# FFN output stores from the scalar engine's queue, x's split pinned in order, and the local attention's way through HBM in two reads

## The chip, the cores and the metric

The kernel runs on one core of a Trainium2 chip. Times are device microseconds (us) of one execution. The engines are PE (matrix products), DVE (VectorE), ACT (ScalarE), POOL (GpSimd) and SP (SyncE, which here does nothing but issue DMA transfers). Each engine works through its own instructions in order.

## The reference

Attention over 8 batches and 8 heads, 576 positions, 64 dimensions, feeds a feed-forward network (FFN) over 4608 tokens:

```python
q_d, k_d, v_d = means over 4 neighbouring positions of q, k, v
out_up    = repeat(softmax(q_d @ k_d.T / 8) @ v_d, 4)             # "far"
mask      = |i - j| < 4
out_local = softmax(where(mask, q @ k.T / 8, -1e9)) @ v           # "local"
x = transpose(out_up + out_local) as (4608, 512)
h = x @ w_in                         # 512 x 2048
r = maximum(h, 0)
out = (s * r * r + b) @ w_out        # 2048 x 512
```

All values are fp32.

## The kernel before

**The FFN** works through 18 tiles of 256 tokens. A tile has 8 panels of 256 hidden columns; a pair (tile, panel) is a step. To keep fp32 accuracy, each operand is split into a high and a low part of the matrix engine's format, and each product is three matmuls: high x high, high x low, low x high. For x these parts are `xh` (a copy with rounding, on ACT) and `xl` (the difference, on DVE), made by `split_x(t)` for a whole tile `t` (L752, L753). A step consists of G, the first products into `ph` (L771); R, on ACT: Relu, Square and the cast to the high part `gh` or `gb` (L786 to L788); V, on DVE: the low part `gl` or the second half of `gb` (L793); and H, the second products into `po` (L852 to L854), which lag G by some three steps. When a tile's H are done, DVE evicts `po` into `os` in two halves (L826), and each half goes to HBM as a store of 128 x 512 values (L829), issued by SP at that place.

**Attention.** The first 28 steps, up to about 240 us, follow an order written out by hand. Behind it a loop emits, per step, some products of G and H, then `finish` (R and V), then a share of the remaining attention (`advance`, a generator that is drawn from as fast as the next batches' x are due), and then `split`, which calls `split_x(t + 1)` once step 5 of tile `t`, for `t` from 3 to 16, is reached. From these emissions a scheduler with a timeline simulation sets each engine's order, so an instruction can stand ahead of where the program emitted it.

The attention left for the loop is that of batches 3 to 7, in ten groups of two head pairs (`two_pairs`), each of two halves. A half of the local part is: seven products `pr` on POOL (L672) of queries with shifted keys, both in `lqk`, a single buffer that is loaded again (768 KB) once the half's last `pr` has read it; seven sums `st` on DVE (L674); a softmax over the seven; and the weighted values, `pv` on DVE (L701), added into `acc` on POOL or DVE (L702). The far part (`tqk`, `qd`, `dmx`, `pd`) runs between these as a chain of its own, whose own transposition goes through HBM too (`away` and `pd`, L605 to L620).

At a group's end the local part has positions on partitions, while x wants model columns there. Two DVE transposes of 32 x 32 blocks (L712) write `ft`, two transfers write that to HBM as `away` (L717, 288 KB each), eight read it back, moved between partitions, into the same `ft` (L722, 72 KB each). POOL then adds the two `ft` into x (L730); these two adds are kept in `late` and emitted behind the last `pr` of the next group's first half. `ft` and `pv` share one pair of buffers. All transfers are issued by SP, in the order of its queue. The words `ft` and `away` name tiles of the far part as well; lines tell them apart.

Of the kernel before, what the change touches and what calls it, by code (L numbers as in the profile page):

```python
# [11 lines left out]
F32 = mybir.dt.float32  # L12
# [4 lines left out]
ALU = mybir.AluOpType  # L17
AX = mybir.AxisListType

P = 128  # L20
# [22 lines left out]
CH = 9  # L43
# [43 lines left out]
def attention_ffn_kernel(ctx, tc, qk, vw_in, vr_in, vdm, qkn, vn, w_in, w_out, s_in, b_in, out):  # L87
    nc = tc.nc
# [3 lines left out]
    def pool(name, bufs, gap=0):  # L92
# [11 lines left out]
    two = pool("two", 2)  # L104
    far_off = ctx.enter_context(
        tc.tile_pool(name="far_off", bufs=2, space=bass.MemoryType.DRAM))
# [5 lines left out]
    def bank(i, shape, name):  # L112
        return ps.tile(shape, F32, tag=f"k{i}", name=name)
# [536 lines left out]
    def two_pairs(b, g, dn):  # L650

        at = GROUPS.index((b, g))
        i = 0

        def far():
            nonlocal i
            if i % 3 == 2:
                next(dn)
            if i == 17:
                load_far(2 * at + 2, ("qk",))  # L660
            i += 1

        acc = None
        st = bank(7, [P, 2, P], "st")
        for h in range(2):
            half = 2 * at + h
            lqk, lv = near_in[half, "lqk"], near_in[half, "lv"]
            ls = take(st[:, h], 0, [P, CH, NO])
            sums = st[:, h, 64 : 64 + CH]
            for o in range(NO):  # L670
                pr = two.tile([P, CH, D], F32, tag="pl", name="pr")
                nc.gpsimd.tensor_tensor(  # L672
                    pr, lqk[:, 0:CH], lqk[:, CH + o : 2 * CH + o], ALU.mult)
                nc.vector.tensor_reduce(ls[:, :, o], pr, AX.X, ALU.add)  # L674
                if o == NO - 1:
                    load_near(half + 1, "lqk")
                    far_values(half)
                    while late:
                        late.pop()()
                far()  # L680
                yield
            row = lambda t: t.unsqueeze(2).to_broadcast([P, CH, NO])
            nc.vector.tensor_tensor(ls, ls, omask, ALU.add)
            lr = two.tile([P, 2, CH], F32, tag="lr", name="lr")
            nc.vector.tensor_reduce(lr[:, 0], ls, AX.X, ALU.max)
            nc.vector.tensor_tensor(ls, ls, row(lr[:, 0]), ALU.subtract)
            nc.scalar.activation(ls, ls, AF.Exp, scale=SCALE)
            nc.vector.tensor_reduce(sums, ls, AX.X, ALU.add)
            nc.vector.tensor_scalar(sums, sums, 1e-9, None, ALU.add)
            nc.vector.reciprocal(lr[:, 1], sums)  # L690
            nc.vector.tensor_tensor(ls, ls, row(lr[:, 1]), ALU.mult)
            far()
            yield
            acc = acc or two.tile([P, CH, 2, D], F32, tag="qk", name="acc")
            for o in range(NO):
                w = ls[:, :, o : o + 1].to_broadcast([P, CH, D])
                if o == 0:
                    nc.vector.tensor_tensor(acc[:, :, h], lv[:, 0:CH], w, ALU.mult)
                else:
                    pv = two.tile([P, CH, D], F32, tag="pv", name="pv")  # L700
                    nc.vector.tensor_tensor(pv, lv[:, o : o + CH], w, ALU.mult)  # L701
                    (nc.vector if o % 3 == 1 else nc.gpsimd).tensor_tensor(  # L702
                        acc[:, :, h], acc[:, :, h], pv, ALU.add)
                if o == NO - 1:
                    load_near(half + 1, "lv")
                far()
                yield
        x = xt[b]
        moved, away = [], []
        for h in range(2):  # L710
            ft = two.tile([P, 2, CH * 32], F32, tag="pv", name="ft")
            nc.vector.transpose(  # L712
                ft.rearrange("p e (i b) -> p e i b", i=CH),
                acc[:, :, h].rearrange("p i (e a) -> p e i a", e=2))
            moved.append(ft)
            away.append(far_off.tile([P, 2, CH * 32], F32, name="away"))
            nc.sync.dma_start(away[h], ft)  # L717
        load_far(2 * at + 3, ("qk",))
        yield
        for u in range(2):  # L720
            for e in range(4):
                nc.sync.dma_start(  # L722
                    moved[u][32 * e : 32 * e + 32],
                    away[e // 2][64 * u : 64 * u + 64, e % 2].rearrange("(r a) n -> a r n", r=2))
        yield

        def add():
            for u in range(2):
                xv = x[:, 2 * g + u].rearrange("p (r b i) -> p r b i", r=2, b=32)
                nc.gpsimd.tensor_tensor(  # L730
                    xv, moved[u].rearrange("p r (i b) -> p r b i", i=CH), xv, ALU.add)
            complete.update((b, 2 * g + u) for u in range(2))

        late.append(add)
        yield
# [4 lines left out]
    def split_x(t):  # L740
        tags = ("os", "xl2") if t == 2 else ("xh", "xl")
        xh, xl = (home[tag].tile([P, HP, TB], F32R, tag=tag, name=name)
                  for tag, name in zip(tags, ("xh", "xl")))
        t0 = t * TB
        while t0 < (t + 1) * TB:
            b = t0 // S
            while (b, HP - 1) not in complete:
                next(gen)
            n = min((t + 1) * TB, (b + 1) * S) - t0
            src = xt[b][:, :, t0 - b * S : t0 - b * S + n]  # L750
            dst = slice(t0 - t * TB, t0 - t * TB + n)
            nc.scalar.copy(xh[:, :, dst], src)  # L752
            nc.vector.tensor_tensor(  # L753
                xl[:, :, dst], src, xh[:, :, dst].bitcast(F32), ALU.subtract)
            t0 += n
        xs[t] = (xh, xl)

# [3 lines left out]
    acc = {}  # L761
# [59 lines left out]
    def evict_half(t, m):  # L821
        if m == 0:
            pool, tag = (xp, "xh") if t < 2 else (xp1, "os")
            held[t] = pool.tile([P, 2, DM], F32, tag=tag, name="os")
        os_ = held[t] if m == 0 else held.pop(t)
        nc.vector.scalar_tensor_tensor(  # L826
            os_[:, m], oacc[t][m], sb_s, bias, ALU.mult, ALU.add)
        r0 = TB * t + P * m
        nc.sync.dma_start(out[r0 : r0 + P, :], os_[:, m])  # L829

    def evict(t):
        for m in range(2):
# [200 lines left out]
                    chain_end = i  # L1033

    def finish(st):
        with tc.high_priority():
            next(streams["R"])
            next(streams["V"])
        advance(st + 0.5)


# [40 lines left out]
    def advance(st):  # L1082
        nonlocal done
        while done < target(st):
            with tc.high_priority(offset=300 if done < NY[1] else 60 if done < NY[1] + NY[2] else 0):
                if next(gen, "end") == "end":
                    break
            done += 1
# [85 lines left out]
```

## Time and profile before

| | |
|---|---|
| median of 3 runs | 943.72 us (942.95 to 945.33) |
| the profiled execution | 944.6 us |
| its span, first to last instruction | 942.8 us |
| granted clock of PE, mean over the span | 0.995 |
| PE, DVE, ACT, POOL busy | 908.2, 654.9, 463.6, 451.8 us |
| bytes moved by DMA | 105.09 MB |
| last instructions of attention | x adds at 780.54 and 782.62 us |

A row of the timeline reads: start, duration, engine, line, operation, output<-input, shape, count, and in brackets how long the engine sat idle before it and what it waited for. In the lists of waits a row reads: who waited, for whom, us in total, times, longest. A row with `SPq` is an issue in SP's queue, and its duration is what the issue took, not the transfer. In the list of transfers the columns are count, size and median us from issue to landing.

### The profile page before, as it was taken

To read this page: it belongs to the slowest core of one execution; us is meant where nothing else is said; L and a number is where in the kernel's file an instruction comes from. 1 tells how busy PE (TensorE), PEld (TensorE's weight loads), DVE (VectorE), ACT (ScalarE), POOL (GpSimd) and SP (SyncE) were. 2 spreads that over 40 slices of the span, in tenths; PEclk is the share of its full clock that TensorE was granted. 3 is DMA by queue.
4 is the path that set the end of the run, shared out by engine and by line. 5 is a ranking of instruction groups with operands and counts; after the bars stand their busy time and mean duration, and the time that the engine had idled before them with its cause. 6 is when DMAs were issued, how large, how long until landed. Compare 5 with 4: busy or idle time off the path is not lost.

```text
span 942.8 us, 18601 instructions
## 1 busy us (share of the span) xinstructions
PE 908.2 (96%) x7106; PEld 815.3 (86%) x7106; DVE 654.9 (69%) x1134; ACT 463.6 (49%) x1073; POOL 451.8 (48%) x461
## 2 busy tenths in 40 slices
PE   6799999999999998999999999999999999999998
PEld 5688888788899888999988988989998989999997
DVE  9999999854588887887888778777968672111111
ACT  7977774466455534454544344345534443233331
POOL 6401120010467878687887677768886831000000
PEclk9999999999999999999999999999999999999999
DMA  9855413123234535434443435154434310000000
GB/s 315 279 163 193 148 47 120 46 88 98 90 113 132 157 100 158 131 118 131 138 148 99 146 101 167 56 181 125 144 100 161 85 61 26 23 1 24 1 23 23
DMA packets 60505, 105.09 MB, mean 111 GB/s; under 512 B 20480, under 2 KB 34048, under 8 KB 60416
## 3 DMA queue, kind: packets, MB, share of 16 engines
q1 hardware_dynamic: 60416, 103.90, 35.1%
q8 instruction: 56, 0.92, 0.4%
q14 instruction: 33, 0.27, 0.1%
HBM read 84.85 MB, written 19.02 MB: 110 GB/s over the span
## 4 chain that ended last, share of the span: by engine, by line
PE 42%; POOL 21%; DVE 15%; DMA 12%; issue 5%; ACT 3%; SPq 2%; DVEq 0%; POOLq 0%; ACTq 0%
PE ph L771 19%; POOL pr L672 11%; POOL acc L702 7%; PE po L852 6%; PE po L853 6%; PE po L854 6%; DMA lqk<-in_qkn_dram 4%; DVE pv L701 2%; DMA tqk<-in_qk_dram 2%; DVE st L674 2%; DMA away<-ft 2%; SPq L722 1%; DVE acc L702 1%; PE ol L481 1%; DMA ft<-away 1%
## 5 line engine op out<-in xcount | busy, mean ns | idle before, releaser
L771 PE MATMUL ph<-xh,wi 128*128 128x256 f32 x2176 | 412.6, 280 | 7.3 <-DVE gl L793 3.9
L771 PEld LDWEIGHTS ph<-xh,wi 128*128 128x128 f32 x2176 | 346.3, 189 | 18.0 <-DVE gl L793 6.1
L771 PE MATMUL ph<-xl,wi 128*128 128x256 f32 x1152 | 321.2, 279 | 0.2
L672 POOL TENSOR_TENSOR pr<-lqk 128x576 f32<-128x576 f32 x140 | 203.9, 1478 | 68.2 <-DMA lqk<-in_qkn_dram 44.3
L771 PEld LDWEIGHTS ph<-xl,wi 128*128 128x128 f32 x1152 | 218.8, 190 | 7.8 <-DVE xl L911 0.4
L786 ACT ACTIVATE ph<-ph 128x512 f32<-128x512 f32 x144 | 83.7, 581 | 258.3 <-PE ph L771 252.7
L852 PE MATMUL po<-wo,gh 128*128 128x512 f32 x416 | 166.7, 401 | 0.3
L854 PE MATMUL po<-wo,gl 128*128 128x512 f32 x416 | 163.1, 392 | 0.8 <-DVE gl L793 0.7
L853 PE MATMUL po<-wo,gh 128*128 128x512 f32 x416 | 163.4, 393 | 0.0
L674 DVE TENSOR_REDUCE st<-pr 128x9 f32<-128x576 f32 x140 | 105.6, 754 | 45.4 <-POOL pr L672 43.9
L702 POOL TENSOR_TENSOR acc<-acc,pv 128x576 f32<-128x576 f32 x80 | 114.7, 1433 | 40.0 <-DVE acc L702 22.7
L793 DVE TENSOR_TENSOR gl<-ph,gh 128x512 fp32r<-128x512 f32 x104 | 70.9, 682 | 85.5 <-ACT gh L788 85.5
L701 DVE TENSOR_TENSOR pv<-lv,st 128x576 f32<-128x576 f32 x120 | 87.8, 747 | 25.7 <-POOL acc L702 21.6
L314 POOL TENSOR_TENSOR dq<-vt 80x64 f32<-80x64 f32 x58 | 21.8, 388 | 174.4 <-PE up L385 172.9
L854 PEld LDWEIGHTS po<-wo,gl 128*128 128x128 f32 x416 | 78.3, 188 | 19.2 <-DVE gl L793 2.1
L852 PEld LDWEIGHTS po<-wo,gh 128*128 128x128 f32 x416 | 78.2, 188 | 13.3 <-issue 0.8
L853 PEld LDWEIGHTS po<-wo,gh 128*128 128x128 f32 x416 | 78.5, 189 | 11.4 <-issue 0.2
L787 ACT ACTIVATE ph<-ph 128x512 f32<-128x512 f32 x144 | 83.8, 582 | 4.0
L788 ACT CAST gh<-ph 128x512 fp32r<-128x512 f32 x104 | 61.1, 587 | 20.3 <-PE po L853 18.2
L852 PE MATMUL po<-wo,gb 128*128 128x512 f32 x160 | 63.2, 395 | 2.9 <-DVE os L826 1.7
L853 PE MATMUL po<-wo,gb 128*128 128x512 f32 x160 | 62.9, 393 | 0.0
L854 PE MATMUL po<-wo,gb 128*128 128x512 f32 x160 | 62.5, 391 | 0.0
(175 smaller groups left out, 1188.4 us busy)
## 6 DMA issues: line engine op xcount, KB each, us to landing
tqk<-in_qk_dram SPq DMA_DIRECT2D x30, 584.0 KB, 4.3
lqk<-in_qkn_dram SPq DMA_DIRECT2D x20, 768.0 KB, 4.4
lv<-in_vn_dram SPq DMA_DIRECT2D x20, 480.0 KB, 3.5
out_dram<-os SPq DMA_DIRECT2D x34, 256.0 KB, 2.1
wst<-in_moe_w_in_dram SPq DMA_DIRECT2D x7, 1024.0 KB, 5.8
wst<-in_moe_w_out_dram SPq DMA_DIRECT2D x7, 1024.0 KB, 5.1
away<-ft SPq DMA_DIRECT2D x20, 288.0 KB, 2.8
ft<-away SPq DMA_DIRECT2D x80, 72.0 KB, 2.0
```

The source lines that it names most:

```text
L672: nc.gpsimd.tensor_tensor(pr, lqk[:, 0:CH], lqk[:, CH + o : 2 * CH + o], ALU.mult)
L674: nc.vector.tensor_reduce(ls[:, :, o], pr, AX.X, ALU.add)
L701: nc.vector.tensor_tensor(pv, lv[:, o : o + CH], w, ALU.mult)
L702: (nc.vector if o % 3 == 1 else nc.gpsimd).tensor_tensor(acc[:, :, h], acc[:, :, h], pv, ALU.add)
L771: nc.tensor.matmul(ph[:, j], wi[p][:, s, k, f], xk[:, k], start=k == 0 and s == 0 and xk is xh, stop=k == NK - 1 and s == 1)
L786: nc.scalar.activation(ph, ph, AF.Relu)
L787: nc.scalar.activation(ph, ph, AF.Square)
L788: nc.scalar.copy(gh, ph)
L793: nc.vector.tensor_tensor(gl, acc.pop((t, p)), gh.bitcast(F32), ALU.subtract)
L852: nc.tensor.matmul(po[m], gh[:, j, ms], wo[p][:, 0, j], start=first, stop=False)
L853: nc.tensor.matmul(po[m], gh[:, j, ms], wo[p][:, 1, j], start=False, stop=False)
L854: nc.tensor.matmul(po[m], gl[:, j, ms], wo[p][:, 0, j], start=False, stop=last)
```

## The change

Three edits.

1. *Stores.* A finished half tile is put on a list, `to_store`. For tiles from the third on, the list is emptied in the next step's `finish`, behind that step's R and V, by DMA issues from ACT's queue, held behind ACT's last emitted instruction by a scheduling dependency (`behind`). The first two tiles' stores, and those of the last tile (another function), stay in SP's queue.
2. *Split.* `xh` is held behind ACT's and `xl` behind DVE's last emitted instruction, so they stay where the program emits them in relation to that.
3. *The local part's return.* One `away` of [4, 128, 288] per group. `turn(h)` transposes half `h` and writes it as four transfers of 72 KB, one for each 32 partitions. It is called for the first half within the second half's `pr` (behind the third), and for the second at the group's end. Two reads of 288 KB then fetch both into two new tiles, `moved`.

```diff
+        away = far_off.tile([4, P, CH * 32], F32, name="away")
+
+        def turn(h):
+            ft = two.tile([P, 2, CH * 32], F32, tag="pv", name="ft")
+            nc.vector.transpose(
+                ft.rearrange("p e (i b) -> p e i b", i=CH),
+                acc[:, :, h].rearrange("p i (e a) -> p e i a", e=2))
+            for r in range(4):
+                nc.sync.dma_start(
+                    away[r, 64 * h : 64 * h + 64].rearrange("(e a) n -> a e n", e=2),
+                    ft[32 * r : 32 * r + 32])
...
+                if h == 1 and o == 2:
+                    turn(0)
...
-        moved, away = [], []
-        for h in range(2):
-            ft = two.tile([P, 2, CH * 32], F32, tag="pv", name="ft")
-            nc.vector.transpose(
-                ft.rearrange("p e (i b) -> p e i b", i=CH),
-                acc[:, :, h].rearrange("p i (e a) -> p e i a", e=2))
-            moved.append(ft)
-            away.append(far_off.tile([P, 2, CH * 32], F32, name="away"))
-            nc.sync.dma_start(away[h], ft)
+        turn(1)
         load_far(2 * at + 3, ("qk",))
         yield
+        moved = []
         for u in range(2):
-            for e in range(4):
-                nc.sync.dma_start(
-                    moved[u][32 * e : 32 * e + 32],
-                    away[e // 2][64 * u : 64 * u + 64, e % 2].rearrange("(r a) n -> a r n", r=2))
+            moved.append(two.tile([P, 2, CH * 32], F32, tag="pv", name="moved"))
+            nc.sync.dma_start(moved[u], away[2 * u : 2 * u + 2].rearrange("r p n -> p r n"))
         yield
...
-            nc.scalar.copy(xh[:, :, dst], src)
-            nc.vector.tensor_tensor(
-                xl[:, :, dst], src, xh[:, :, dst].bitcast(F32), ALU.subtract)
+            with behind(nc.scalar.engine):
+                nc.scalar.copy(xh[:, :, dst], src)
+            with behind(nc.vector.engine):
+                nc.vector.tensor_tensor(
+                    xl[:, :, dst], src, xh[:, :, dst].bitcast(F32), ALU.subtract)
...
-        nc.sync.dma_start(out[r0 : r0 + P, :], os_[:, m])
+        to_store.append(((nc.sync if t < 2 else nc.scalar), out[r0 : r0 + P, :], os_[:, m]))
+        if t < 2:
+            store(1)
+
+    to_store = []
+
+    def store(count):
+        for _ in range(count):
+            engine, dst, src = to_store.pop(0)
+            engine.dma_start(dst, src)
...
     def finish(st):
+        ready = len(to_store)
         with tc.high_priority():
             next(streams["R"])
             next(streams["V"])
+            with behind(nc.scalar.engine):
+                store(ready)
         advance(st + 0.5)
```

The change adds 12 lines ahead of L672, so lines move: `pr` is L684 behind it, the x add L735, `xh` L758, the casts L795, the stores L845, the writes L673, the reads L729.

How the scheduler's orders differ is shown at three places. The first is POOL's queue in the first half of the second group: that half's `pr`, `vt` of the far part, the first group's two adds into x, then `pr` of the next half, whose `lqk` is loaded behind the last `pr` of this one. Before:

```order
L672 TENSOR_TENSOR pr<-lqk 128x576 x4
L310 TENSOR_TENSOR vt<-tvd 80x256
L672 TENSOR_TENSOR pr<-lqk 128x576
L730 TENSOR_TENSOR x<-ft,x 128x576 x2
L672 TENSOR_TENSOR pr<-lqk 128x576 x2
L702 TENSOR_TENSOR acc<-acc,pv 128x9x64
```

And with the change:

```order
L684 TENSOR_TENSOR pr<-lqk 128x576 x4
L735 TENSOR_TENSOR x<-moved,x 128x576 x2
L684 TENSOR_TENSOR pr<-lqk 128x576
L310 TENSOR_TENSOR vt<-tvd 80x256
L684 TENSOR_TENSOR pr<-lqk 128x576 x2
L315 TENSOR_TENSOR dq<-vq 64x64 x2
```

The two adds (`x`) have moved from behind the half's last `pr` to ahead of it.

The second is SP's queue at the end of the first group, from the local part's last write to the load of the next `lqk`. Before (the rows of L717 and L722 are the local part's, those of L609, L614 and L620 the far part's):

```order
L717 DMA away<-ft 128x576
L722 DMA ft<-away 32x2x288 x2
L717 DMA away<-ft 128x576
L609 DMA away<-ft 96x288
L609 DMA away<-ft 96x192
L722 DMA ft<-away 32x2x288 x6
L614 DMA pd<-away 32x3x96
L636 DMA lqk<-in_qkn_dram 128x1536
L614 DMA pd<-away 32x3x96
L614 DMA pd<-away 16x3x96
L620 DMA pd<-away 32x3x48 x4
```

And with the change:

```order
L673 DMA away<-ft 32x2x288 x4
L729 DMA moved<-away 128x2x288
L609 DMA away<-ft 96x288
L729 DMA moved<-away 128x2x288
L609 DMA away<-ft 96x192
L614 DMA pd<-away 32x3x96 x2
L614 DMA pd<-away 16x3x96
L620 DMA pd<-away 32x3x48 x4
L636 DMA lqk<-in_qkn_dram 128x1536
```

Eight reads have become two, and the `lqk` load now stands behind all reads of `pd`. The four writes of the group's first half now stand further up, after an earlier `lv` load:

```order
L636 DMA lv<-in_vn_dram 128x960
L673 DMA away<-ft 32x2x288 x4
L156 DMA tqk<-in_qk_dram 128x1168
L156 DMA tvr<-in_vr_dram 128x256
L636 DMA lqk<-in_qkn_dram 128x1536
L609 DMA away<-ft 96x288
```

The third is ACT's queue around the split of the tile with index 6 (its first piece, 192 tokens), by the softmax's exponential `st` of the same half as a mark. Before:

```order
L788 CAST gb<-ph 128x512
L786 ACTIVATE ph<-ph 128x512
L752 CAST xh<-x 128x4x192
L787 ACTIVATE ph<-ph 128x512
L788 CAST gh<-ph 128x512
L687 ACTIVATE st<-st 128x63
L786 ACTIVATE ph<-ph 128x512
L787 ACTIVATE ph<-ph 128x512
```

And with the change:

```order
L845 DMA out_dram<-os 128x512 x2
L793 ACTIVATE ph<-ph 128x512
L794 ACTIVATE ph<-ph 128x512
L795 CAST gh<-ph 128x512
L701 ACTIVATE st<-st 128x63
L793 ACTIVATE ph<-ph 128x512
L794 ACTIVATE ph<-ph 128x512
L795 CAST gb<-ph 128x512
L793 ACTIVATE ph<-ph 128x512
L794 ACTIVATE ph<-ph 128x512
L795 CAST gh<-ph 128x512
L758 CAST xh<-x 128x4x192
```

`xh` stood ahead of `st` and within a step; it now stands two steps behind `st`, after a step's cast. The two stores of a finished tile stand between two steps, each issued once its half is in `os`; with the waits listed, each also waits for one of eight DMA semaphores, which ACT's stores share with SP's transfers: the one transfer that used the semaphore last must have landed.

## The prediction

> **What bounds the kernel now.** I read the busy table first, then the chain of work that ended last, then what the matmul engine (PE) waited for, then single instructions around those waits. The busy row and the chain:
>
> ```profile
> PE 908.2 (96%) x7106; PEld 815.3 (86%) x7106; DVE 654.9 (69%) x1134; ACT 463.6 (49%) x1073; POOL 451.8 (48%) x461
> PE 42%; POOL 21%; DVE 15%; DMA 12%; issue 5%; ACT 3%; SPq 2%; DVEq 0%; POOLq 0%; ACTq 0%
> ```
>
> PE is busy for 908.2 of 942.8 us, so 34.6 us is everything a change of order could win. The chain runs through attention (POOL, DVE, DMA) all the same: while attention and FFN share the chip, some of PE's products wait for an x that is late. The change touches the time from 240 us on, when the hand-written plan is over, and in that stretch PE's waits are few:
>
> ```profile
> PE ph L771 <- DVE gl L793: 3.9, 3, 2.3
> PE ph L771 <- ACT xh L752: 2.6, 1, 2.6
> PE po L852 <- DVE os L826: 1.7, 1, 1.7
> PE up L547 <- ACT ph L786: 1.4, 2, 0.7
> PE po L852 <- DVE dsm L596: 1.2, 1, 1.2
> PE up L547 <- DMA pd<-away: 0.6, 1, 0.6
> PE ph L771 <- DVE gb L793: 0.6, 1, 0.6
> ```
>
> Columns: total us, times, longest, for 240 to 790 us. They sum to 12.0 us. Behind 790 PE never waits:
>
> ```profile
> 360.00:384.00 24.00, 21.26 (x124) 18.87 (x124) 17.59 (x33) 9.23 (x18) 17.05 (x13) 0.93 0.42 121
> 792.00:816.00 24.00, 24.00 (x162) 21.96 (x162) 5.44 (x7) 8.11 (x14) 0.00 (x0) 1.00 0.06 23
> ```
>
> Columns: length, busy PE, PEld, DVE, ACT, POOL, granted clock. The first window has a second loss, a clock of 0.93 behind the wait for xh:
>
> ```profile
> 369.00:372.00 3.00, 3.00 (x17) 2.91 (x16) 2.86 (x7) 0.00 (x0) 0.31 (x1) 0.63 1.04 341
> 372.00:375.00 3.00, 3.00 (x21) 2.87 (x20) 1.72 (x3) 1.35 (x3) 3.00 (x3) 0.81 0.19 75
> 621.00:624.00 3.00, 1.79 (x6) 1.60 (x7) 2.90 (x6) 0.00 (x0) 1.10 (x1) 0.72 0.50 170
> 624.00:627.00 3.00, 3.00 (x20) 2.90 (x20) 2.92 (x5) 0.00 (x0) 2.39 (x3) 0.71 0.51 136
> ```
>
> Lost at the first place: 3 x 0.37 + 3 x 0.19 = 1.7 us; at the second 3 x 0.28 + 3 x 0.29 = 1.7. These follow PE's two longest waits (2.6 and 2.3 us); so each of the two is worth about 4 us, not 2.5. [...]
>
> So at most 12.0 + 2 x 1.7 = 15.4 us can be won, and each microsecond that an x comes later at a place with no slack is lost in full.
>
> **Term 1, the stores.** 30 stores (15 tiles x 2) go from SP's queue to ACT's, behind the next step's casts. ACT's room (its wait for PE between 240 and 790), and ACT at the one long wait of its own that I tie to PE:
>
> ```profile
> ACT ph L786 <- PE ph L771: 157.3, 64, 7.2
> 541.15 0.20 ACT L589 ACTIVATE dmx<-dmx 96x3 f32<-96x3 f32 x1 [4.46 <-DVE dmx L588]
> 548.28 0.39 PE L771 MATMUL ph<-xh,wi 128*128 128x256 f32 x1 [1.30 <-DVE gl L793]
> ```
>
> ACT pays an issue each, 0.37 us by the rows below, 30 x 0.37 = 11 us, and these lie in the 157.3 us: cost 0, with the cover gone 0.37 us a store. But ACT's queue is in order, and the order of the change shows each store waiting for the last user of its DMA semaphore, mostly a transfer of SP's. Behind a store stand the next step's Relu, Square and Cast and so PE's products. ACT's 4.46 us at 541 put the two Relu, Square and Cast behind it late, and PE lost 1.30 us at 548.28. Bounds 0 and 3 such places, 3.9; I take +0.5, nearer to 0 since a store comes a whole step after its tile is evicted. The room in SP's queue is the gain:
>
> ```profile
> 624.96 1.43 POOL L672 TENSOR_TENSOR pr<-lqk 128x576 f32<-128x576 f32 x1
> 626.25 0.37 SPq L829 DMA_DIRECT2D out_dram<-os  x1
> ...
> 627.69 0.37 SPq L829 DMA_DIRECT2D out_dram<-os  x1
> 628.11 3.25 SPq L722 DMA_DIRECT2D ft<-away  x7
> 631.46 0.37 SPq L636 DMA_DIRECT2D lqk<-in_qkn_dram  x1
> ```
>
> POOL's last pr ends at 626.39; the load of the next lqk could go then, and goes 5.1 us later, behind two stores and eight reads. This is the worst of the ten groups. With 2 reads and no stores ahead of it some 4 us come back, here, to attention. [...]
>
> But x is not late after 622. One wait for x reaches PE, at 367.83; four more stay on ACT (next term). So this 4 us moves no PE product: 0 on the path, unless x comes to be late there.
>
> **Term 2, x's split.** Before, the scheduler put xh ahead of its place where ACT had room, and ACT then sat waiting for POOL's x:
>
> ```profile
> ACT xh L752 <- POOL x L730: 14.7, 5, 6.6
> L753 DVE TENSOR_TENSOR xl<-x,xh 128x1024 fp32r<-128x1024 f32 (+3 forms) x19 | 25.3, 1337 | 11.7 <-ACT xh L752 11.6
> ```
>
> Pinned behind step 5 of the tile before, both come later and these waits shrink. What of it reaches PE: xl at 513.38 (1.32 us) stood ahead of the gb for which PE waited 0.6 us (the last row of PE's waits). The other two rows are for term 4:
>
> ```profile
> 513.38 1.32 DVE L753 TENSOR_TENSOR xl<-x,xh 128x1024 fp32r<-128x1024 f32 x1
> ...
> 620.18 0.75 DVE L529 TENSOR_REDUCE qd<-tqk 128x144 f32<-128x576 f32 x1 [1.75 <-DMA tqk<-in_qk_dram]
> ...
> 622.21 0.48 PE L771 MATMUL ph<-xh,wi 128*128 128x256 f32 x1 [2.29 <-DVE gl L793]
> ```
>
> I take -0.6. From below -1.3 (the 548 wait too), from above +1.3: a pinned xl can stand ahead of another gl.
>
> **Term 3, the local part's return.** Issues per group stay 10, 4 + 4 writes and 2 reads for 2 writes and 8 reads, but behind the last transpose only 6 are left. By the 0.37 to 0.46 us (3.25 / 7) of an issue above, the last read goes some 4 x 0.4 = 1.6 us sooner. Where does that help? Only where POOL's x waits for it, and at PE's one wait for x it does not:
>
> ```profile
> 359.80 2.82 POOL L672 TENSOR_TENSOR pr<-lqk 128x576 f32<-128x576 f32 x2
> 362.58 1.75 POOL L730 TENSOR_TENSOR x<-ft,x 128x576 f32<-128x576 f32 x1
> ...
> 365.64 1.70 POOL L730 TENSOR_TENSOR x<-ft,x 128x576 f32<-128x576 f32 x1
> 367.37 1.35 ACT L752 CAST xh<-x 128x256 fp32r<-128x256 f32 x2 [2.97 <-POOL x L730]
> 367.83 0.38 PE L771 MATMUL ph<-xh,wi 128*128 128x256 f32 x1 [2.59 <-ACT xh L752]
> ```
>
> No DMA is named ahead of the x adds: POOL is full with pr, and x comes when its place in POOL's order comes. So an earlier read gives 0 here, and what decides is when POOL gets this far. That is set one group earlier, and there the order changes against the kernel: the two x adds of the first group, behind the last pr before, now stand ahead of it.
>
> ```profile
> 306.35 0.74 DVE L712 STREAM_TRANSPOSE ft<-acc 128x576 f32<-128x576 f32 x1
> 312.22 1.44 POOL L672 TENSOR_TENSOR pr<-lqk 128x576 f32<-128x576 f32 x1
> 313.61 4.14 POOL L730 TENSOR_TENSOR x<-ft,x 128x576 f32<-128x576 f32 x2
> 319.72 3.29 POOL L672 TENSOR_TENSOR pr<-lqk 128x576 f32<-128x576 f32 x2 [1.97 <-DMA lqk<-in_qkn_dram]
> lqk<-in_qkn_dram SPq DMA_DIRECT2D x20, 768.0 KB, 4.4
> away<-ft SPq DMA_DIRECT2D x20, 288.0 KB, 2.8
> ft<-away SPq DMA_DIRECT2D x80, 72.0 KB, 2.0
> ```
>
> The last pr (312.22) frees lqk's only buffer. Before, the adds ran while the next lqk was on its way; now they run ahead of its load. The way of it: the last transpose ends at 307.1; four writes issue in 1.6 us and land 2.0 (72 KB) to 2.8 us later; two reads of 288 KB issue in 0.8 and land 2.0 to 2.8 later: the first x add starts, 0.4 ahead of the second's data, between 313.1 and 314.7. Two adds of 1.75, the pr 1.4, the load 4.4: the next pr starts at 322.4 to 324.0, 2.7 to 4.3 us behind 319.72. POOL's rows up to 367 then stand much as before, so PE's wait for x becomes 2.6 + 2.7 to 2.6 + 4.3. I take +3.5. Below, 0, if the attention chain has room before 367 that I don't see.
>
> Later groups have the same flip (x adds ahead of a half's last pr: 4 of 20 before, 9 after; 5 x 1.75 = 8.8 us of cover lost), against which stands SP's relief (the 4 us of the seventh group). After 368 the x adds end well ahead of their tiles' first products, so I count 0 for both.
>
> **Term 4, shuffled waits.** DVE's and POOL's order changes nearly everywhere, and the rest of the 12.0 us (gl 3.9 with its 1.7 of clock, os 1.7, up 2.0, dsm 1.2: 10.5) hangs on which DVE instruction stands ahead of a gl or an eviction. The wait at 622 had gl behind the reduce qd, which itself waited 1.75 us for a load. Such a meeting is drawn again. Between -10.5 and about as much again I take a quarter off, -2.5: the load queue that made the dearest one gets shorter.
>
> **Sum**, against the profiled execution (944.6, its span 942.8 plus 1.8): 944.6 + 0.5 - 0.6 + 0 + 3.5 - 2.5 = 945.5. The median shown, 943.72, is 0.9 below that execution, so 944.6 in its terms; I say 944.5, no change.
>
> **The rivals.**
>
> *A, x waits no more.* Were x's adds released by the transfers, or the first half's earlier send to take the first group's pipeline along, the 2.6 us at 367.83 goes with its 1.7 of clock, the 0.56 with it, and the 622 wait by SP's relief with its clock (2.3 + 1.7): -8.9, 934.8; with one of the two places alone -4.5, 939. For it: the reads do land sooner, SP has 5.1 us to give. Against it: the rows at 362 to 367 name no DMA. Chance 0.34.
>
> *B, lqk behind the x adds.* The upper end of term 3 and nothing from term 4: POOL's x adds of the first group delay the load by 4.3 us, the wait at tile 6 becomes 6.9, and its half clock lasts for one window more (+1.7): 943.7 + 4.3 + 1.7 = 949.7. It decides once the reads land later than POOL is done with the four pr ahead of the adds. For it: the order is fixed and POOL cannot pass a waiting add. Against it: DVE reduces those pr meanwhile, and a later half may catch up. Chance 0.21.
>
> *C, ACT stuck at a store.* Three or four stores wait over 4.5 us for a transfer of SP's and PE pays 1.3 each: 943.7 + 5 = 948.7. Against it: ACT waited 6.6 us for x at one place before with no wait of PE behind it. Chance 0.08.
>
> **How the numbers follow.** 0.3% (2.8 us) is about what a measurement here can tell from no change. Forecast 0.37, A 0.34, B and C 0.29: faster 0.35, same 0.36, slower 0.29 with the forecast's own edges. The range reaches to the end of A and of B, 935 to 950; the forecast's own is 941 to 947.
>
> **What would show it.** Right: PE's wait for xh at tile 6 is longer than 2.6 us; in the first group POOL shows x, then pr, then a wait for lqk of more than 1.97 us; SP's gap of 5.1 us from a last pr to its lqk load falls under 2; ACT's issue of stores shows no PE wait within 6 us. Wrong: xh's wait gone (A), or a row of ACT waiting for a DMA ahead of a Relu that PE waits for (C).

## The result, and the profile after it

The changed kernel took 950.9 us (median of 4 runs, 950.38 to 951.79) against 943.9 us before: 1.0074 times as long, 95% interval 1.0056 to 1.0091. Measured again beside other kernels it was 950.23 us against 944.51, 1.0062 (1.0044 to 1.0080). The forecast was 944.5 and no change, the range 935 to 950: the change is slower by 6 to 7 us, just outside the range. Rival B, at 949.7, came nearest. A second profile of the changed kernel is used below as well.

The page of the changed kernel: busy times, chain, and two groups.

```profile
PE 907.8 (96%) x7106; PEld 815.3 (86%) x7106; DVE 652.9 (69%) x1134; ACT 463.0 (49%) x1073; POOL 451.4 (48%) x461
...
PE 41%; POOL 24%; DVE 16%; DMA 12%; issue 5%; SPq 1%; ACT 1%; DVEq 0%; POOLq 0%; ACTq 0%
...
L684 POOL TENSOR_TENSOR pr<-lqk 128x576 f32<-128x576 f32 x140 | 205.2, 1487 | 73.2 <-DMA lqk<-in_qkn_dram 53.8
...
L716 POOL TENSOR_TENSOR acc<-acc,pv 128x576 f32<-128x576 f32 x80 | 115.2, 1440 | 49.5 <-DVE acc L716 34.3
```

No engine has more to do: PE 907.8 us where it had 908.2, DVE 652.9 for 654.9. What grew is waiting. POOL's wait for `lqk` went from 44.3 to 53.8 us, and POOL's share of the chain from 21 to 24%. What PE waited for from 240 to 800 us (before: 12.0 us in all):

```profile
PE ph L778 <- ACT xh L758: 4.7, 1, 4.7
PE ph L778 <- DVE gb L800: 3.2, 3, 1.3
PE po L868 <- DVE os L833: 3.1, 3, 2.5
PE up L547 <- DMA pd<-away: 1.9, 2, 1.2
PE ph L778 <- DVE gl L800: 1.5, 2, 0.9
PE ph L778 <- DVE xl L760: 1.2, 2, 0.6
PE po L868 <- ACT ph L793: 0.7, 1, 0.7
PE up L547 <- issue: 0.2, 1, 0.2
```

That is 16.5 us. The windows say where. Before and after, 300 to 390, 390 to 660 and 660 to 801 us (length, then PE's busy time; the granted clock is the third value from the end of a row):

```profile
300.00:390.00 90.00, 86.42 (x561) 78.46 (x561) 71.93 (x124) 41.19 (x103) 71.53 (x67) 0.98 0.44 134
390.00:660.00 270.00, 263.43 (x1723) 238.63 (x1722) 215.29 (x373) 120.70 (x294) 207.59 (x183) 0.99 0.42 129
660.00:801.00 141.00, 138.69 (x918) 126.21 (x917) 96.88 (x166) 61.35 (x139) 87.84 (x77) 1.00 0.31 96
```

```profile
300.00:390.00 90.00, 82.79 (x527) 74.92 (x526) 70.64 (x117) 36.95 (x89) 68.46 (x61) 0.96 0.39 121
390.00:660.00 270.00, 264.94 (x1758) 240.78 (x1757) 211.99 (x368) 122.62 (x295) 209.60 (x188) 1.00 0.43 130
660.00:801.00 141.00, 136.73 (x898) 123.35 (x897) 100.49 (x176) 61.69 (x147) 89.38 (x79) 1.00 0.34 102
```

Adding the busy time spent at half clock, taken from windows of 3 us (as in the prediction: length times the missing clock), PE lost what the table shows. In the traces of before and after the clock is either 1.00 or 0.50, and from 240 to 800 us it is 0.50 in four stretches of 3.41 us each: before from 369.76 and 622.34 us on, with the change from 336.98 and 374.53. Such a stretch, 1.7 us of lost clock, is a half-clock window in what follows.

| us lost by PE: idle + half clock | before | after | after, second profile |
|---|---|---|---|
| 300 to 390 | 3.6 + 1.7 | 7.2 + 3.4 | 9.2 + 3.4 |
| 390 to 660 | 6.6 + 1.7 | 5.1 + 0 | 4.7 + 0 |
| 660 to 802 | 2.3 + 0 | 4.3 + 0 | 3.7 + 0 |
| sum | 15.9 | 20.0 | 21.0 |
| span | 942.8 | 948.8 | 947.4 |

Some 5.3 to 7.3 us are lost in one stretch, 3.2 to 3.6 come back in the next, and 1.4 to 2.0 go at the end. (Half clock that falls into a wait is counted twice here; in the second profile's 3.4 us that is some 0.6, an estimate from the windows around 373.) The first after-profile also started 2.1 us late (first eviction of `os` at 181.03 where before had 178.92); in the second the start is level within 0.4 us, and the span is still 4.6 us longer than before.

The stretch from 300 to 390 step by step. Where the four `pr` of the second group's first half started before:

```profile
305.85 5.59 POOL L672 TENSOR_TENSOR pr<-lqk 128x576 f32<-128x576 f32 x4
```

And the timeline of the changed kernel. POOL, then SP, then the two waits of PE with what released them:

```profile
307.90 5.60 POOL L684 TENSOR_TENSOR pr<-lqk 128x576 f32<-128x576 f32 x4
313.88 4.01 POOL L735 TENSOR_TENSOR x<-moved,x 128x576 f32<-128x576 f32 x2 [0.37 <-DMA moved<-away]
317.84 1.43 POOL L684 TENSOR_TENSOR pr<-lqk 128x576 f32<-128x576 f32 x1
319.30 0.36 SPq L636 DMA_DIRECT2D lqk<-in_qkn_dram  x1
324.50 3.34 POOL L684 TENSOR_TENSOR pr<-lqk 128x576 f32<-128x576 f32 x2 [4.53 <-DMA lqk<-in_qkn_dram]
...
332.42 0.76 DVE L715 TENSOR_TENSOR pv<-lv,st 128x576 f32<-128x576 f32 x1 [0.97 <-POOL acc L716]
336.31 0.73 DVE L833 SCALAR_TENSOR_TENSOR os<-po,sb_s,bias 128x512 f32<-128x512 f32 x1
337.19 0.77 PE L868 MATMUL po<-wo,gh 128*128 128x512 f32 x1 [2.46 <-DVE os L833]
...
372.49 1.68 POOL L735 TENSOR_TENSOR x<-moved,x 128x576 f32<-128x576 f32 x1
374.21 0.40 ACT L758 CAST xh<-x 128x256 fp32r<-128x256 f32 x1 [5.65 <-POOL x L735]
374.66 0.58 PE L778 MATMUL ph<-xh,wi 128*128 128x256 f32 x1 [4.75 <-ACT xh L758]
```

From the start of the four `pr` to the next half's first `pr` it took 319.72 - 305.85 = 13.9 us before, and takes 324.50 - 307.90 = 16.6 now: 2.7 us more. The two adds and the last `pr` stand ahead of the load, and the 4.53 us in which `lqk` is on its way are bare. PE meets this delay at two places. At 374.66 it waits 4.75 us for `xh` where it waited 2.59. And at 337.19, where it had not waited, it waits 2.46 us for an eviction: on DVE the `os` stands behind `pv`, and that one waits for POOL's `acc`, which is as late as the `pr`. In this profile each of the two has a half-clock window behind it.

The two waits are not two prices, though. In every profile here the same 3437 products of PE stand ahead of tile 6's first one, and that one starts when its `xh` is there. Counted from the start of the four `pr`, this was 367.83 - 305.85 = 61.98 us before, and is 374.66 - 307.90 = 66.76 us now. In the second profile of the change it is 66.76 us again, though PE's waits on the way are divided otherwise (3.06 us for `os` without half clock behind it, then 6.12 us for `xh`). Between 337 and 374 no wait of POOL or DVE names PE, and DVE's two for ACT are of 0.19 and 0.27 us. So what PE lost at 337 was taken off its wait at 374, and the lateness of x, 4.8 us, sets the sum. Of these, 2.7 to 2.9 us are the delay of the load. The other 2 are lost later on POOL: from the next half's first `pr` to the end of the second add into tile 6's x it took 367.34 - 319.72 = 47.6 us before, and takes 374.17 - 324.50 = 49.7 now (49.5 in the second profile), as POOL idles 9.8 us there for 8.0, nearly all of the difference in waits for DVE's `acc`, `pv` and `st`. From tile 6's first product to the last instruction the changed kernel takes 574.1 and 574.0 us, where before took 575.0: the whole loss lies ahead of that product.

### The profile page after: what moved, and what is told of

Read it like the earlier page. It is cut to its first block, busy times and chain, and to the rows that moved or that the text cites. A ratio compares the mean times of both kernels' runs of the same rounds, so it can differ in the third digit from the quotient of the medians.

```text
span 948.8 us, 18529 instructions
## 1 busy us (share of the span) xinstructions
PE 907.8 (96%) x7106; PEld 815.3 (86%) x7106; DVE 652.9 (69%) x1134; ACT 463.0 (49%) x1073; POOL 451.4 (48%) x461
## 4 chain that ended last, share of the span: by engine, by line
PE 41%; POOL 24%; DVE 16%; DMA 12%; issue 5%; SPq 1%; ACT 1%; DVEq 0%; POOLq 0%; ACTq 0%
PE ph L778 18%; POOL pr L684 12%; POOL acc L716 8%; PE po L868 6%; PE po L870 6%; PE po L869 6%; DMA lqk<-in_qkn_dram 5%; DVE pv L715 2%; DMA away<-ft 2%; DVE st L686 2%; POOL x L735 1%; DVE acc L716 1%; DMA tqk<-in_qk_dram 1%; PE ol L481 1%; DVE es L274 1%
## 5 line engine op out<-in xcount | busy, mean ns | idle before, releaser
L684 POOL TENSOR_TENSOR pr<-lqk 128x576 f32<-128x576 f32 x140 | 205.2, 1487 | 73.2 <-DMA lqk<-in_qkn_dram 53.8
L716 POOL TENSOR_TENSOR acc<-acc,pv 128x576 f32<-128x576 f32 x80 | 115.2, 1440 | 49.5 <-DVE acc L716 34.3
L795 ACT CAST gh<-ph 128x512 fp32r<-128x512 f32 x104 | 61.1, 588 | 23.8 <-PE po L869 21.8
```

The lines of the kernel that those rows point to most:

```text
L684: nc.gpsimd.tensor_tensor(pr, lqk[:, 0:CH], lqk[:, CH + o : 2 * CH + o], ALU.mult)
L716: (nc.vector if o % 3 == 1 else nc.gpsimd).tensor_tensor(acc[:, :, h], acc[:, :, h], pv, ALU.add)
L795: nc.scalar.copy(gh, ph)
```

## The experiments

Theory 1: the x adds ahead of the last `pr` delay the next `lqk`, and PE pays near 337 and 374. Theory 2: the pinned split costs. Theory 3: the stores on ACT cost. Medians, ratio to the kernel before measured beside it, the time from the start of the four `pr` to the next half's first `pr` and to tile 6's first product, and what PE lost from 300 to 390 (idle + half clock, as above):

| run | us | ratio (95%) | x adds ahead of last `pr`, first group | 4 `pr` to next half, us | 4 `pr` to tile 6, us | 300 to 390 lost |
|---|---|---|---|---|---|---|
| stores only | 942.25 | 0.9975 (0.9956 to 0.9993) | 0 | 14.0 | 61.4 | 4.9 |
| stores only, again | 943.43 | 0.9983 (0.9967 to 0.9999) | 0 | 13.6 | 62.0 | 5.6 |
| stores, return, x behind | 945.52 | 1.0007 (0.9993 to 1.0021) | 0 | 13.8 | 62.0 | 4.5 |
| all, x behind | 946.33 | 1.0021 (1.0003 to 1.0040) | 0 | 14.6 | 63.7 | 7.7 |
| split, x behind | 951.16 | 1.0067 (1.0046 to 1.0089) | 0 | 14.2 | 62.4 | 7.5 |
| split only | 948.00 | 1.0029 (1.0009 to 1.0048) | 1 | 15.5 | 63.3 | 8.6 |
| return only | 946.74 | 1.0026 (1.0012 to 1.0041) | 1 | 16.1 | 65.6 | 10.8 |
| all (the change) | 950.23 | 1.0062 (1.0044 to 1.0080) | 2 | 16.7 | 66.8 | 12.6 |
| before, x ahead | 957.87 | 1.0130 (1.0103 to 1.0157) | 2 | 18.7 | 66.7 | 13.1 |

The kernel before has 13.9, 62.0 and 5.3 in the last three columns. They rise with the adds ahead of the last `pr`: without one 4.5 to 7.7 us are lost there, with one 8.6 to 10.8, with both 12.6 to 13.1 (10.6 in the first profile of the change). The five runs told further below have no add ahead either; four of them lost 4.1 to 6.4 us, and one 8.4, with a wait of its own at 325. The whole time does not follow these columns alone: what the pinned split costs lies elsewhere, as the runs below show.

**All, with the first group's x adds held back.**

```diff
                 if o == NO - 1:
+                    last_pr = next(
+                        i for i in reversed(nc.cur_bb.bb.instructions) if i.engine == nc.gpsimd.engine)
                     load_near(half + 1, "lqk")
                     far_values(half)
-                    while late:
-                        late.pop()()
+                    with behind(nc.gpsimd.engine, last_pr) if half == 2 else contextlib.nullcontext():
+                        while late:
+                            late.pop()()
```

> The changed kernel with one edit: the first group's two x adds are held behind the last pr of the half in which they run, as in the kernel before; all else stays in the program, though the scheduler draws later groups again. Theory 1 (the x adds ahead of the last pr hold back the next lqk load, the attention chain runs 2.7 us later against PE, and PE pays three times in the next 50 us: 2.5 us for os, 1.7 us of half clock behind it, 2.1 us more for xh): about 950.9 - 6.3 = 944.6, between 942 and 947, with the next pr within 1 us of its place before and no wait for os above 1 us near 337. Theory 2 (the pinned split costs it) and theory 3 (the stores on ACT cost it): 950.9, within 1.5 us.

946.33 us, 3.9 below the change (950.23 when it was run again, by ratios 1.0021 for 1.0062): theory 1, though 1.7 above its mark. Its timeline:

```profile
306.92 5.60 POOL L684 TENSOR_TENSOR pr<-lqk 128x576 f32<-128x576 f32 x4
314.35 1.43 POOL L684 TENSOR_TENSOR pr<-lqk 128x576 f32<-128x576 f32 x1 [1.83 <-DVE st L686]
315.74 3.43 POOL L738 TENSOR_TENSOR x<-moved,x 128x576 f32<-128x576 f32 x2
321.52 2.97 POOL L684 TENSOR_TENSOR pr<-lqk 128x576 f32<-128x576 f32 x2 [1.66 <-DMA lqk<-in_qkn_dram]
...
335.44 0.47 PE L871 MATMUL po<-wo,gh 128*128 128x512 f32 x1 [0.51 <-DVE os L836]
370.64 0.38 PE L781 MATMUL ph<-xh,wi 128*128 128x256 f32 x1 [4.04 <-ACT xh L761]
```

The adds cover the load again (1.66 us bare for 4.53), the wait for `os` is 0.51 for 2.46. The wait for `xh` stayed at 4.04, so theory 1's count of that part (2.1 us back) was wrong. It had charged the two waits side by side; since x sets the sum, tile 6 alone is enough: its first product comes 63.7 us behind the four `pr`, 3.0 sooner than with the change and 1.7 later than before. Part of these 1.7 is lost in the second group's second half, where POOL's `vt` of the far part stands ahead of the last `pr` and waits 1.12 us for a transfer.

**Before, with the x adds ahead.** The kernel before, with the first group's adds emitted ahead of that half's last `pr`, and this held behind them.

```diff
+                flip = half == 2 and o == NO - 1
+                if flip:
+                    while late:
+                        late.pop()()
                 pr = two.tile([P, CH, D], F32, tag="pl", name="pr")
-                nc.gpsimd.tensor_tensor(
-                    pr, lqk[:, 0:CH], lqk[:, CH + o : 2 * CH + o], ALU.mult)
+                with behind(nc.gpsimd.engine) if flip else contextlib.nullcontext():
+                    nc.gpsimd.tensor_tensor(
+                        pr, lqk[:, 0:CH], lqk[:, CH + o : 2 * CH + o], ALU.mult)
```

> The kernel before with one edit: in the first half of the second group the two x adds are emitted ahead of the last pr, and that pr is held behind them; stores, split and return are as before. Theory 1: the next lqk load starts some 5 us later, PE's wait for xh at tile 6 grows by 2 to 5 us and a wait for os may come: 946.5 to 951. Theories 2 and 3: 943.9, within 1.5 us.

957.87 us, more than any theory gave. Without stores, split or return changed, the two waits of the changed kernel stand at the same places:

```profile
324.59 2.82 POOL L677 TENSOR_TENSOR pr<-lqk 128x576 f32<-128x576 f32 x2 [5.75 <-DMA lqk<-in_qkn_dram]
...
335.43 0.77 PE L857 MATMUL po<-wo,gh 128*128 128x512 f32 x1 [2.36 <-DVE os L831]
372.66 0.58 PE L776 MATMUL ph<-xh,wi 128*128 128x256 f32 x1 [4.61 <-ACT xh L757]
...
528.93 0.58 PE L776 MATMUL ph<-xh,wi 128*128 128x256 f32 x1 [5.00 <-DVE gb L798]
```

From 300 to 390 it lost 13.1 us, 7.8 more than before, and tile 6's first product comes 4.7 us later behind the four `pr`, all of it at the load (18.7 us for 13.9). Another 8.0 us are lost behind that product, with the wait at 528.93 and three half-clock windows between 525 and 648 (5.1 us). Nothing forecast them: PE's order is nearly that of before, but this one edit drew DVE's again at some fifty places, far beyond its own.

**Stores only.** Of the change, the edits of `evict_half`, `store` and `finish`. This alone leaves POOL's order as it was up to 725 us, and DVE's up to 635.

> The kernel before with only the stores moved to ACT's queue. POOL's order is then that of before in every half. Theory 1: 943.9 within 1.5 us, up to 1 us faster by SP's relief. Theory 3: 948 to 951, with ACT waiting at a store ahead of a Relu that PE waits for.

942.25, and 943.43 when measured again below: 0.2% faster, both intervals just below 1. Theory 3 falls. In the list of ACT's waits from 240 to 790 the stores have one row:

```profile
ACT ph L786 <- DMA out_dram<-os: 4.8, 3, 1.6
```

Three waits of 1.6 us at most, and none of PE's waits in this kernel names ACT's Relu, Square or cast. The room in SP's queue is real, and small: the load of the seventh group's `lqk` goes at 627.30, right behind the eight reads and not behind two stores as well, 4.1 us after POOL's last `pr` for 5.1 before.

**Split only**, and **split with the x adds held behind** (the edit of the first run):

> The kernel before with only the split pinned on ACT and DVE. POOL's order then has one of the first group's x adds ahead of the last pr (before: none), so theory 1 expects the lqk load 1.75 us later and 944 to 948. Theory 2 expects 949 to 951, with waits of PE for xl or behind it.

> The split pinned alone, with the first group's x adds held behind the last pr. If theory 1 explains all of the 4 us that the split alone lost, 943 to 945, within 1.2 us of before. If the pinned split costs by itself (xl ahead of a low part, a shuffled DVE), 946.5 to 949.

948.00, at the upper edge of theory 1, and 951.16. Holding the adds back mended its place (14.2 us for 15.5, 7.5 lost for 8.6) and the time got longer, not shorter: the expectation of 943 to 945 failed, and for the split by itself theory 2 holds beside theory 1. So two runs asked which pin it is. Each has the stores on ACT, the x adds held behind, and one pin.

> Stores on ACT; of the split only xh is pinned (ACT), xl is left to the scheduler; the first group's x adds are held behind the last pr. The split pinned whole had waits of PE for xl (2.1 and 2.7 us near 759) with half clock behind them. If pinning xl on DVE is what costs: as the stores alone, 941 to 944, no wait for xl above 1 us. If pinning xh costs (a later xh holds xl back): 946 to 949.

> As the run with xh pinned, but only xl is pinned (DVE) and xh is left to the scheduler. If pinning xl costs: 946 to 949, with PE waiting for xl near 759. If pinning xh costs: 941 to 944.

952.15 (1.0077, 1.0057 to 1.0096) and 950.77 (1.0069, 1.0050 to 1.0088): both cost 8 to 9 us against the stores alone, so each pin costs, and more than expected. The loss lies behind tile 6's first product: from there to the end they take 580.7 and 580.4 us, where before took 575.0. In the run with `xl` pinned the reason can be read. DVE, then PE:

```profile
757.00 0.76 DVE L674 TENSOR_REDUCE st<-pr 128x9 f32<-128x576 f32 x1 [0.61 <-POOL pr L672]
...
758.36 0.76 DVE L674 TENSOR_REDUCE st<-pr 128x9 f32<-128x576 f32 x1
759.03 1.22 DVE L757 TENSOR_TENSOR xl<-x,xh 128x1024 fp32r<-128x1024 f32 x1
...
760.30 0.58 PE L775 MATMUL ph<-xl,wi 128*128 128x256 f32 x1 [4.22 <-DVE xl L757]
```

In the kernel before, this tile's `xl` was made 50 us earlier:

```profile
707.14 1.21 DVE L753 TENSOR_TENSOR xl<-x,xh 128x1024 fp32r<-128x1024 f32 x1
```

Pinned, it stands behind sums that wait for POOL's `pr`, and comes when PE already waits. From 660 to 802 PE lost 13.1 us in this run, 8.7 with `xh` pinned, 9.2 and 6.6 in the two with the split pinned, and 2.3 before. With `xh` alone pinned PE has no wait for `xl` there, but waits for `os`, `gl` and `pd`; why these came was not read. In the changed kernel it is 4.3 and 3.7; there this `xl` is made at 761.16, and PE waits 0.6 us for it.

**Return only**, and **stores and return with the x adds held behind**, the first half sent early or not:

> The kernel before with only the local part's new way through HBM (four writes a half, the first half early, two reads). POOL's order then has one of the first group's x adds ahead of the last pr. Theory 1: the next pr starts 1 to 2 us later than before, as with the split alone (1.6 us there): 944.5 to 948. If the new return is a gain in itself that outweighs it: 941 to 943.5.

> The kernel before with the stores on ACT and the new return, without the pinned split, and with the first group's x adds held behind the last pr. Theory 1: no loss in the first group, the stores' gain of about 2 us kept: 940 to 943. If the new return costs by itself: 944 to 947.

> Stores on ACT and the new return, without the pinned split, the first group's x adds behind the last pr, and both halves turned at the group's end (none early). With the first half early, 1.8 us of PE's waits for os stood near 336 and 2.4 near 434. If the early transpose, standing on DVE ahead of an eviction, costs these: 941 to 943.5. If the early half gains by emptying the group's end: 945.5 to 948.

946.74 for the return alone, as theory 1 had it. 945.52 for stores and return with the adds held back, above the 940 to 943 expected and within the 944 to 947 for a return that costs by itself: theory 1's place is clean (13.8 us, 4.5 lost), but of the stores' 2 us nothing is left. PE waits 1.78 us for `os` near 336 and 2.43 near 434, where the early transpose stands on DVE near an eviction. Without the early half the first of these stayed (1.71), so the transpose is not its cause; the second is gone, and yet 950.48 came out (1.0057, 1.0036 to 1.0077), with new waits of 2.84 and 2.93 us for `gl` at 479 and 625. These orders differ in too many places to put a price on the early half. It is left open.

Stores and return with the adds held back, and all edits with the adds held back, differ by the split's pin alone: 1.0007 and 1.0021, or 1.3 us, with intervals that overlap. So the pin, which costs 6 us by itself, can't be told from nothing beside the stores and the return.

**The change again:**

> The changed kernel itself, beside the others of this call. Theory 1 needs its loss to be there again: 949 to 952 against a kernel before at 943 to 944.5, with the wait for lqk of 4 to 5 us behind the first group's x adds, PE's wait for os near 337 and for xh near 374. If PE's wait for os (2.5 us with its 1.7 us of half clock) is a matter of the single execution, it is missing here, and 946 to 948 stands in place of 950.9.

Both waits are there, and so is the time, 950.23 us. No half clock stands behind the first wait here; both half-clock windows (3.4 us) stand at the second.

```profile
336.20 0.47 PE L868 MATMUL po<-wo,gh 128*128 128x512 f32 x1 [3.06 <-DVE os L833]
373.49 0.58 PE L778 MATMUL ph<-xh,wi 128*128 128x256 f32 x1 [6.12 <-ACT xh L758]
```

**Attention of batch 3 emitted earlier**, one number (5 to 12 steps ahead of the tile), with the stores on ACT:

> The kernel before with the stores on ACT and one number changed: the attention of batch 3, the first whose x the loop has to bring, is emitted to be done 12 steps ahead of its tile in place of 5. If what PE loses at tile 6 (2 to 3 us of waiting for xh and 1.7 us of half clock in the stores-only kernel) is that the attention chain starts too late for it, the wait for xh goes and 938 to 940.5 stands in place of 942.25, without new waits before 390. If the chain is bound by POOL and the load of lqk from its first instruction, the order changes nothing or crowds DVE: 942 to 946.

946.33 us (1.0012, 0.9997 to 1.0027). PE's wait for `xh` stayed (1.98 us), and one of 2.92 us for a product that stands behind POOL's `pr` came at 325. The 938 to 940.5 of an earlier start did not come; the time is just above the 942 to 946 of a chain that is bound from its first instruction. That it is bound so fits, and is not shown.

**The second group's x adds ahead.** The same flip at the place where it should pay: the adds of the x for which PE waits at tile 6, with the stores on ACT. PE's order does not change, POOL's there and for one `pr` near 385, and DVE's at some fifteen places.

> The kernel with the stores alone on ACT, once more, beside the next run: its gain of 0.25% was near the edge of its interval. If it is a gain: ratio 0.996 to 0.999. If it was drawn luck: 0.999 to 1.002.

> The stores alone on ACT, and in the first half of the third group, where the adds of the second group's x stand (the x that PE waits for at tile 6), both adds go ahead of the last pr, which is held behind them; PE's order does not change at all, POOL's only there. The same flip that cost at the first group: here the second add comes 1.4 us sooner, and the delayed lqk load can harm only later tiles, whose x have room. Theory 1, in its full form (what counts is whether x or the next lqk is late for PE): the wait for xh at tile 6 (1.9 us in the stores-only kernel) falls by 1 to 1.4 us, and with it at times its 1.7 us of half clock, 1 to 3 us faster than stores alone: 939 to 941.5. If x adds ahead of a last pr cost wherever they stand: 944 to 947.

944.25 us (0.9995, 0.9981 to 1.0009) beside 943.43 for the stores alone. The place did what theory 1 said:

```profile
364.07 3.45 POOL L735 TENSOR_TENSOR x<-ft,x 128x576 f32<-128x576 f32 x2
...
368.02 0.38 PE L776 MATMUL ph<-xh,wi 128*128 128x256 f32 x1 [0.51 <-ACT xh L757]
...
433.43 0.47 PE L866 MATMUL po<-wo,gb 128*128 128x512 f32 x1 [1.88 <-ACT gh L793]
```

The wait for `xh` fell from 1.93 to 0.51 us, and the half clock behind it is gone (granted clock 1.00 from 300 to 390, for 0.98 in the stores alone). Then it was given back: PE's waits of 0.69 and 1.88 us near 430 are new, in the stretch behind the delayed `lqk`; that the load makes them is not shown. 944.25 is just inside the 944 to 947 of the second outcome, but beside 943.43 it is no loss that these runs can tell, and the 1 to 3 us of the first were not gained.

## Why the prediction was wrong

**Read rightly.** The flip of the first group's x adds, found in the order and priced at 2.7 to 4.3 us, is there and measures 2.7 to 2.9. SP's gap ahead of the seventh group's `lqk` fell from 5.1 us to 0.4 (POOL's `pr` end at 630.59, the load goes at 630.94), and it moved no product of PE, as said. ACT's stores made no wait of PE. The wait for `gl` at 622 with its half clock is gone, and the one at 548; the stretch from 390 to 660 gained 3.2 to 3.6 us.

**Term 3, mis-sized: the step that failed most.** It had the mechanism, the load behind the x adds, and this part of x's lateness measured 2.7 to 2.9 us, the low end of its 2.7 to 4.3. The step that failed is "POOL's rows up to 367 then stand much as before": POOL lost 2 us more on the way to tile 6's x, so x came 4.8 us late and not 3.5. In the run with the flip alone this stretch takes 47.6 us as before, so the 2 us come from the order that the other edits drew, not from the flip. Tile 6's first product then came 5.3 us later in the second profile, counted from level starts, with one more half-clock window at its wait; in the first it came 6.8 us later, of which 2.1 are the late start. Term 3 also left out DVE, which serves both sides from one queue: PE met part of the delay at an eviction (`os` at 336.31, 2.46 us of waiting) behind a late `pv` (332.42). That changed where PE waited and not how much, since x came no later by it.

**Rival B** had this mechanism with the larger size: 6.9 us of waiting at tile 6 and one half-clock window more there. The second profile shows 6.12 and that window, with 3.06 at 337 ahead of it. But its 4.3 us at the load measured 2.7 to 2.9, so that its 949.7 lies near the result is partly luck. Its +1.7 was the clock lost at 369 and at 622 before, counted once more; that a longer wait at tile 6 brings one more half-clock window stood in no view of before. Behind the 4.75 us of the first profile there is one, at the 6.12 us of the second there are two.

**Term 2, not borne out.** It took -0.6 to -1.3 for pinning the split, since a wait on ACT would go. On ACT it went (5.7 us in one wait for 14.7 in five), but no gain from it reached PE: the wait at 516 that was to go is 1.1 us now (526.79), behind a sum that waits for POOL's `pr`. By itself, with the x adds held back, the split costs 1.0067. What the scheduler's freedom bought was lead: `xl` up to 50 us ahead of its product. The bound of +1.3 looked for the harm behind `xl`, in a `gl` that it would hold up; in three of the four runs with a pin and without the return there is a wait of 2.1 to 4.2 us for `xl` itself. In the changed kernel these waits are 0.6 us each, and the pin's price there is the 1.3 us that can't be told from nothing.

**Term 4, half right.** -2.5 for waits drawn anew was -3.2 to -3.6 up to 660, and +1.4 to +2.0 behind it, where the sum had nothing. Terms 1, 2 and 4 together forecast -2.6; from tile 6's first product on, -0.9 and -1.0 came.

**Term 1, a little wrong.** +0.5 for the stores; alone they gain 0.2% (1.5 to 2 us). Which wait that comes from isn't settled: the waits of PE in its two profiles differ (10.7 and 12.0 us idle, 12.6 before).

So the loss of 6 to 7 us is made up as follows, each step between two runs and by their ratios: the stores -2.0, the return +2.6 beside them (with the x adds held back; the intervals just touch), the split's pin +1.3 (not clear of noise), and the first group's order +3.9. These are prices in this order alone: the pin without the return costs 6 us. Shown with its way to PE is the 3.9; where the return's 2.6 come from is open.

The stores alone are faster than the kernel before by 0.2%, at the edge of what these runs can tell.

## What to carry to other kernels

When a compiler's order changes, follow the late chain up to the operand that the matmul engine waits for, and add up how late that operand is. Waits on the way, as here the 2.46 us at an eviction that stands behind a late `pv` in DVE's queue, are a part of that lateness and not a second payment, as long as the operand does not come later by them. A transfer that fills a buffer again waits for its last reader (here the load of `lqk` went 0.03 us behind the half's last `pr`, at 319.30), so work that needs no part of the buffer belongs behind that reader, where it covers the load (4.53 us of waiting with the x adds ahead, 1.66 with them behind). And an operation that an order places long ahead of its use is a cushion; pinning it to its logical place can sell the cushion for waiting time on an engine that had time to wait (here 14.7 us of ACT's waits for x became 5.7). An edit's price by itself is not its price beside others: here the pin cost 6 us alone and 1.3 beside the other edits.

## What the runs showed of the hardware

Behind waits of much the same length PE's clock was halved or was not. Stores alone, second profile, a wait of 1.93 us for `xh` at 368.50, and the window behind it; then stores and return, a wait of 2.43 us for `os` at 434.04:

```profile
369.00:372.00 3.00, 2.96 (x11) 2.67 (x12) 2.43 (x6) 0.51 (x2) 0.00 (x0) 0.50 0.82 270
```

```profile
435.00:438.00 3.00, 3.00 (x26) 2.92 (x26) 2.96 (x6) 0.26 (x1) 1.37 (x1) 1.00 0.41 154
```

Half clock behind the shorter wait (0.50 from 369 to 372), none behind the longer (1.00 from 432 to 441). So the length of a wait alone did not tell whether clock was lost here; what did is not shown. Where some 2 us of idle stood, 0 or 1.7 us more was the price.

The traces of before and after have each of their half-clock windows from 240 to 800 us at one of PE's longest waits: before at those of 2.59 us (ended at 367.83) and 2.29 us (622.21), with the change at those of 2.46 us (337.19) and 4.75 us (374.66). PE's next longest wait there was 1.67 us before, for `os` at 723.06, with a clock of 1.00 from 720 to 726, and 1.3 us with the change, with no half clock in the trace between 378 and 800 us.

At the program's start half clock cost less. In the first profile of the change the clock was 0.50 from 24 to 36 us, where the kernel before had 1.00:

```profile
24.00:36.00 12.00, 6.71 (x35) 5.14 (x33) 11.59 (x28) 11.47 (x31) 5.79 (x10) 0.50 0.98 348
```

PE idled for 5.3 of these 12 us, with the DMA engines at 0.98, so much of the lost clock fell into waiting. The first eviction came 2.1 us later than before in this profile; with the same clock there it came 0.3 us later in the second profile of the change, 0.6 later in the first of the stores alone, and level in the second. What made the 2.1 us is not shown.
